# A long convolution with a gate: in the last phase the sums run eight rows ahead of the taps in place of ten

## The chip, the cores and the metric

The kernel runs on one core of one Trainium2 chip. The metric is the device time of one execution in microseconds (us); the time given for a kernel is the median of its timed runs. A profiled execution of its own gives the trace, with times from the start of the span.

## The reference

```
# attention part: u = x*v is convolved along the sequence (12800 long) with a filter from a small MLP
h_filt = (np.maximum(pos_emb @ w1, 0.0) @ w2) * np.exp(-0.01 * pos)[:, None]
y = irfft(rfft(x * v, n=2*S, axis=1) * rfft(h_filt, n=2*S, axis=0), n=2*S, axis=1)[:, :S]
x = x * y                                    # (4, 12800, 128)
# gate part, five taps along the sequence
xp = np.concatenate([np.zeros((B, 4, D)), x], axis=1)
gate_pre = sum(conv_w[k] * xp[:, k:k + S] for k in range(5))
return ((1 / (1 + np.exp(-gate_pre))) * (x @ w_val)) @ w_out
```

## The kernel before

Three phases stand one behind the other. The first transforms the input and the filter, the second multiplies the spectra and goes halfway back, and both leave their results in DRAM. The last phase, from about 684 us to the end, is the one that the change touches: it finishes the inverse transform row by row, multiplies with x, and runs the gate part. The sequence is cut in 2 halves (`j`) of 64 rows; a row is a tile of 128 channels x 400 values (4 batches x 100 positions). Four rows are a group; there are 32 groups (`t` = 0 to 31, `g` = 0 to 15 in each half), so 128 rows.

The order of all instructions on each engine is the order of the program text (`tc.manual_schedule()`): one loop over steps `i`, with `t, r = divmod(i, 4)`, so that a step is "row r of group t" for the taps. One step issues, in this order:

- `y_trans` (TensorE, then ScalarE): four transposes of a summed row into PSUM (`tp`, L684), and two ScalarE copies from it (`dif`, L686 and L687);
- `value` (TensorE, L728) for row r of group t-1, then `finish_last` (ScalarE copy `o_sb`, L746) and `project_last` (TensorE, L738) for the rows ahead of it;
- in even steps `y_sum` for two rows (TensorE, `sd`, L672);
- `tap(t, r + 1)` (VectorE, L716): `gt` = `ext` rows * weight + `gt`, 128x1600, over the four rows that end with row r of group t;
- `gated` (VectorE, `gd`, L733), the value row times the sigmoid;
- `y_join`: VectorE adds `tp` and `dif` to `yr` (L697), and GpSimd multiplies `yr` with x into a row of the buffer `ext` (L699);
- `y_copy` (ScalarE, `sd_sb`, L677);
- at certain r, on ScalarE: `fill_halo` (L655 to L657 or L659), `tap(t + 1, 0)` (L713, 128x1600), and at r = 3 `sigmoid(t)` (`sg`, L721).

`LEAD` sets how many steps the sums stand ahead: row number n (counted in the order in which rows are summed) is summed at step n - LEAD, and transposed and joined two steps later (`LAG`). The rows are summed with the last group of a half first (it goes to the buffer `tail`), so row r of group t is row number 4(t + 1) + r, but for the last group of each half.

`ext` is a buffer of 20 rows, two in turn: 4 rows of halo, then the 16 rows of four groups. Taps 0 to 4 of a group read `ext` rows that start k = 0 to 4 rows below its own; so the first group of a buffer reads the halo rows, which are the last four rows of the buffer before. `fill_halo` copies these on ScalarE (L659, 128x1600) for the second to fourth buffer of a half; for the first of a half it builds them from the tails in three or four smaller copies.

Of the kernel before, what the change touches and what calls it, by code (L numbers as in the profile page):

```python
# [29 lines left out]
R = 4  # L30
# [88 lines left out]
def tile_longconv_gate(  # L119
# [326 lines left out]
    def load_part(s, c, i):  # L446
        j, g = y_order[s]
        if (s, c) not in rows_in:
            rows_in[s, c] = buffer(NP + 1 + s)
        k0, n, step, p0 = PARTS[i]  # L450
        to = rows_in[s, c][p0:p0 + step * (n - 1) + 1:step]
        m, n0 = divmod(g * R, H2)
        if j == 0:
            n0 += m * N2 + c * H2
            nc.sync.dma_start(out=to, in_=c_y[k0:k0 + n, n0:n0 + R].rearrange("k p e -> k (p e)"))
        else:
            if m:
                n0 = H2 - R - n0
            nc.sync.dma_start(
                out=to.rearrange("k (q f) -> k q f", q=2),  # L460
                in_=c_z[k0:k0 + n, m, :, c, n0:n0 + R].rearrange("k q i e -> k q (i e)"))
# [152 lines left out]
    with tc.tile_pool(name="p3", bufs=1, reuse_waits="tile") as p3, \  # L614
# [4 lines left out]
        EG = 4  # L619
        assert HALO == R  # L620
        groups = [(j, g) for j in range(J) for g in range(NG)]
        tails, exts, loads3, sds, tps, gate_sg, gate_gt, outs3 = {}, {}, {}, {}, {}, {}, {}, {}

        def load_x(s):
            j, g = y_order[s]
            xr = p3.tile([D, R * ROW], F32, name="xr", bufs=3)
            nc.sync.dma_start(out=xr, in_=xt[j][:, g * R:(g + 1) * R].rearrange("d n b a -> d (n b a)"))
            loads3[s] = xr

        def load_rows(s, parts):  # L630
            for c in range(2):
                for i in parts:
                    load_part(s, c, i)
            if s not in loads3:
                load_x(s)
# [7 lines left out]
        def new_ext(j, q):  # L643
            e = p3.tile([D, HALO + EG * R, B, N1], F32, name="ext", bufs=2)
            exts[j, q] = e
# [15 lines left out]
        def y_sum(s, r):  # L661
            sd = ps3.tile([128, B * D], F32, name="sd", bufs=2)
            j, g = y_order[s]
            m = g * R // H2
            for c in range(2):
                to, t = sd[c * N2:(c + 1) * N2], rows_in[s, c]
                if j == 0:
                    t = t[:, r * B * D:(r + 1) * B * D]
                else:
                    t = t.rearrange("k (q i e) -> k q i e", q=2, i=R)[:, :, R - 1 - r if m else r]  # L670
                    to = to.rearrange("k (q e) -> k q e", q=2)
                nc.tensor.matmul(out=to, lhsT=inv[:, 2 if j * m * c else c], rhs=t, start=True, stop=True)  # L672
            sds[s, r] = sd
# [6 lines left out]
        def y_trans(s, r):  # L680
            t = sds.pop((s, r))
            tp = ps3.tile([D, B, 128], F32, name="tp3", bufs=2)
            for b in range(B):
                nc.tensor.transpose(out=tp[:, b], in_=t[:, b], identity=ident)  # L684
            dif = p3.tile([D, B, 2, NH], F32, name="dif", bufs=3)
            nc.scalar.copy(out=dif[:, :, 0], in_=tp[:, :, N2:N2 + NH])  # L686
            nc.scalar.activation(dif[:, :, 1], tp[:, :, N2 + 1:N2 + NC1], AF.Copy, scale=-1.0)  # L687
            tps[s, r] = tp, dif
# [11 lines left out]

        def rows(t, k=HALO):
            j, g = groups[t]
            e = exts[j, g // EG].rearrange("d n b a -> d (n b a)")
            r0 = g % EG * R + k
            return e[:, r0 * ROW:(r0 + R) * ROW]

        ALL, TWO = slice(0, R * ROW), (slice(0, 2 * ROW), slice(2 * ROW, R * ROW))
# [1 line left out]
        def tap(t, k, cols=ALL):  # L709
            if k == 0:  # L710
                gt = p3.tile([D, R * ROW], F32, name="gt", bufs=2)
                gate_gt[t] = gt
                nc.scalar.activation(gt, rows(t, 0), AF.Copy, scale=cw[:, 0:1])  # L713
            else:
                gt = gate_gt[t][:, cols]
                nc.vector.scalar_tensor_tensor(gt, rows(t, k)[:, cols], cw[:, k:k + 1], gt, op0=ALU.mult, op1=ALU.add)  # L716
# [6 lines left out]
        def value(t, r):  # L723
            if t == NT - 1 and r >= 2:
                v_ps = ps3.tile([128, B * D], F32, name="sd", bufs=2)[:, 0:ROW]
            else:
                v_ps = ps3.tile([D, ROW], F32, name="v_ps", bufs=2)
            nc.tensor.matmul(out=v_ps, lhsT=wval, rhs=rows(t)[:, r * ROW:(r + 1) * ROW], start=True, stop=True)  # L728
            return v_ps
# [21 lines left out]
                nc.scalar.dma_start(  # L751
                    out=out[j][:, g * R + r0:g * R + r1].rearrange("d n b a -> d (n b a)"), in_=o_sb[:, r0 * ROW:r1 * ROW])

        NT, LEAD, LAG = len(groups), 10, 2
        y_run, gd_last, o_last = [], None, None

        def project_last():
            nonlocal gd_last, o_last
            if gd_last is not None:
                o_last = gd_last[0], gd_last[1], project(gd_last[2])  # L760
                gd_last = None

        def finish_last():
            nonlocal o_last
            if o_last is not None:
                finish(*o_last)
                o_last = None

        with tc.manual_schedule():
            load_x(0)  # L770
            for c, i in ((0, 2), (1, 2)):
                load_part(0, c, i)
            for c, i in ((0, 1), (1, 1), (0, 2), (1, 2)):
                load_part(1, c, i)
            load_x(1)
            for c, i in ((0, 1), (0, 2), (1, 0), (1, 1), (1, 2)):
                load_part(2, c, i)
            load_x(2)

            for i in range(-LEAD, (NT - 1) * R):  # L780
                t, r = divmod(i, R)
                s, q = divmod(i + LEAD, R)
                if q == 0 and s < NT:
                    if 3 <= s + 1 < NT:
                        load_rows(s + 1, (0, 1, 2))
                    j, g = y_order[s]
                    if g == NG - 1:
                        tails[j] = p3.tile([D, R, B, N1], F32, name="tail", bufs=2)
                    elif g % EG == 0:
                        new_ext(j, g // EG)  # L790
                done = y_run.pop(0) if len(y_run) == LAG or s >= NT and y_run else None
                if done:
                    y_trans(*done)
                v_ps = value(t - 1, r) if t >= 1 else None
                finish_last()
                project_last()
                if s < NT and q % 2 == 0:
                    y_sum(s, q)
                    y_sum(s, q + 1)
                if t >= 0:  # L800
                    tap(t, r + 1)
                if v_ps is not None:
                    gd_last = t - 1, r, gated(t - 1, r, v_ps)
                if done:
                    y_join(*done)
                if s < NT:
                    y_copy(s, q)
                    y_run.append((s, q))
                if t + 1 >= 0:
                    j, g = groups[t + 1]  # L810
                    if r == 0 and g == NG - 1:
                        nc.scalar.copy(out=exts[j, g // EG][:, EG * R:], in_=tails[j])
                    if r == 1 and g % EG == 0:
                        fill_halo(j, g // EG)
                    if r == 2:
                        tap(t + 1, 0)
                if t >= 0 and r == R - 1:
                    sigmoid(t)

            t = NT - 1  # L820
            v_last = []
            for i, (h, k) in enumerate((h, k) for h in range(2) for k in range(1, KC)):
                if i < R:
                    v_ps = value(t - 1, i)
                finish_last()
                project_last()
                if i in (R, R + 1):
                    v_last += [value(t, len(v_last)), value(t, len(v_last) + 1)]
                tap(t, k, TWO[h])
                if i < R:  # L830
                    gd_last = t - 1, i, gated(t - 1, i, v_ps)
                elif i in (6, 7):
                    gd_last = t, i - 6, gated(t, i - 6, v_last[i - 6])
                if k == KC - 1:
                    sigmoid(t, TWO[h])
            finish_last()
            project_last()
            for r in (2, 3):
                gd_last = t, r, gated(t, r, v_last[r])
                finish_last()  # L840
                project_last()
            finish_last()
# [41 lines left out]
```

## Time and profile before

| | |
|---|---|
| median of 3 timed runs | 1064.03 us (1063.89 to 1065.49) |
| the profiled execution's own time | 1066.52 us |
| its span in the trace | 1064.7 us |
| mean granted clock of TensorE | 0.976 |
| busy, share of the span: TensorE / VectorE / GpSimd / ScalarE | 92% / 91% / 70% / 61% |
| median to profiled execution | the median is 2.49 us below it |

The busy shares are averages over three phases. What this change is worth is read from the last phase alone. A record's length is not always the distance to the next one on its engine: VectorE and ScalarE start an instruction a little before the record of the one ahead has ended, so steps are measured here from start to start.

### The profile page before, as it was taken

The numbers are of one execution on the slowest core, as the hardware profiler recorded it, in microseconds if no ns is written. First come the engines' busy times: TensorE is split into PE (matmuls) and PEld (weight loads), VectorE is DVE, ScalarE is ACT, GpSimd is POOL, SyncE is SP. The second block draws the span as 40 slices with busy tenths as digits, with TensorE's granted clock in tenths as the row PEclk, the third lists the DMA queues.
The fourth block names the chain that finished last, engine by engine and source line by source line (L and its number), as shares of the span: only waits on it lengthen the run. The fifth ranks groups of instructions, "written<-read, shape, count | busy, mean of one in ns | idle before, by whom it ended". The sixth has DMA issues, their size and how long they took to land.

```text
span 1064.7 us, 21554 instructions
## 1 busy us (share of the span) xinstructions
PE 978.8 (92%) x8100; PEld 515.6 (48%) x8100; DVE 966.9 (91%) x933; ACT 649.2 (61%) x1145; POOL 747.9 (70%) x465
## 2 busy tenths in 40 slices
PE   2778799999988999999999999689999999999996
PEld 0344466566644545555445545334444444444442
DVE  8878999699948999999989999369999999999997
ACT  1445577788852444444444434277887888878784
POOL 2232222222225999999899999679999999999990
PEclk9989899999997999999999999899999999999999
DMA  8999899988989889989999997977888888888813
GB/s 286 383 352 375 330 381 373 397 315 327 393 273 306 318 302 334 341 314 339 333 311 342 345 334 259 333 285 270 312 286 300 284 295 306 282 299 296 299 72 124
DMA packets 97152, 330.16 MB, mean 310 GB/s; under 512 B 12691, under 2 KB 37883, under 8 KB 81051
## 3 DMA queue, kind: packets, MB, share of 16 engines
q1 hardware_dynamic: 41864, 196.96, 54.1%
q10 hardware_dynamic: 49506, 111.30, 27.0%
q0 software_dynamic: 5680, 20.53, 5.1%
q8 instruction: 66, 1.08, 0.4%
q14 instruction: 36, 0.29, 0.1%
HBM read 197.67 MB, written 131.07 MB: 309 GB/s over the span
## 4 chain that ended last, share of the span: by engine, by line
PE 65%; DMA 13%; DVE 7%; POOL 5%; ACT 4%; issue 4%; SPq 1%; ACTq 1%; DVEq 0%; POOLq 0%
PE sd L672 11%; PE o_ps L738 8%; PE v_ps L728 7%; PE c_ps L531 7%; PE fp L392 6%; PE tp L684 6%; PE c_ps L508 6%; PE z_ps L492 5%; DMA xv<-in_xv_dram 4%; DMA ld<-in_xv_dram 3%; PE gp L293 3%; PE ap L267 3%; DMA c_z<-c_both 2%; DVE vb L498 2%; POOL c_both L543 2%
## 5 line engine op out<-in xcount | busy, mean ns | idle before, releaser
L699 POOL TENSOR_TENSOR ext<-yr,xr 128x400 f32<-128x400 f32 x120 | 308.3, 2570 | 23.2 <-DVE yr L697 10.8
L716 DVE SCALAR_TENSOR_TENSOR gt<-ext,cw,gt 128x1600 f32<-128x1600 f32 (+1 forms) x132 | 242.3, 1835 | 0.1
L401 POOL DMA_DIRECT2D a_u<-st x62 | 33.3, 537 | 222.9 <-ACT st L393 219.1
L393 ACT COPY st<-fp 128x1024 f32<-128x1024 f32 x124 | 125.7, 1029 | 81.6 <-PE fp L392 41.4
L672 PE MATMUL sd<-ld,inv 128*64 128x512 f32 x512 | 128.0, 619 | 7.2 <-DMA ld<-c_y 6.7
L543 POOL TENSOR_TENSOR c_both<-c_raw 128x512 f32<-128x512 f32 x100 | 126.6, 1295 | 9.9 <-DMA c_z<-c_both 6.4
L536 ACT COPY c_raw<-c_ps 128x1024 f32<-128x1024 f32 x50 | 50.8, 1015 | 135.3 <-PE c_ps L531 117.9
L498 DVE TENSOR_TENSOR va<-z_ps,h_sb 128x2048 f32<-128x2048 f32 x50 | 114.1, 2282 | 19.7 <-PE z_ps L492 19.6
L579 POOL TENSOR_TENSOR va<-va,vb 128x1024 f32<-128x1024 f32 x49 | 117.0, 2387 | 20.4 <-DVE vb L498 20.4
L498 DVE TENSOR_TENSOR vb<-z_ps,h_sb 128x2048 f32<-128x2048 f32 x50 | 114.2, 2284 | 12.8 <-POOL va L582 12.8
L492 PE MATMUL z_ps<-ld,ld 64*64 64x512 f32 x800 | 111.6, 614 | 10.2 <-DVE vb L498 6.1
L392 PE MATMUL fp<-ld,fsd 64*128 64x512 f32 x320 | 89.4, 663 | 27.3 <-DVE ld L343 14.5
L738 PE MATMUL o_ps<-gd,wout 128*128 128x400 f32 x256 | 107.8, 503 | 6.1 <-DVE gd L733 4.6
L677 ACT COPY sd_sb<-sd 128x512 f32<-128x512 f32 x128 | 76.9, 601 | 49.4 <-PE sd L672 37.8
L728 PE MATMUL v_ps<-ext,wval 128*128 128x400 f32 x252 | 105.4, 501 | 0.0
L508 PE MATMUL c_ps<-va,ld 64*64 64x512 f32 x800 | 98.1, 604 | 4.0 <-POOL va L579 2.5
L582 POOL TENSOR_TENSOR va<-va,vb 128x1024 f32<-128x1024 f32 x42 | 101.0, 2406 | 0.0
L684 PEld LDWEIGHTS tp<-ident,sd_sb 128*128 128x128 f32 x512 | 58.3, 140 | 77.8 <-PE sd L672 45.4
L697 DVE TENSOR_TENSOR yr<-tp,dif 128x400 f32<-128x400 f32 x128 | 72.5, 566 | 25.8 <-ACT dif L687 21.6
L514 ACT COPY c_sb<-c_ps 128x1024 f32<-128x1024 f32 x49 | 49.7, 1014 | 59.5 <-PE c_ps L508 59.5
L684 PE MATMUL tp<-ident,sd_sb 128*128 128x128 f32 x512 | 80.0, 280 | 4.0 <-DVE yr L697 4.0
L733 DVE TENSOR_TENSOR gd<-v_ps,sg 128x400 f32<-128x400 f32 x126 | 71.4, 567 | 0.2 <-ACT sg L721 0.2
(116 smaller groups left out, 1817.7 us busy)
## 6 DMA issues: line engine op xcount, KB each, us to landing
ld<-a_u SPq DMA_DIRECT2D x48, 1024.0 KB
a_u<-st ACTq DMA_DIRECT2D x61, 512.0 KB
xr<-in_xt_dram SPq DMA_DIRECT2D x32, 800.0 KB
c_y<-c_sb ACTq DMA_DIRECT2D x49, 512.0 KB
out_dram<-o_sb ACTq DMA_DIRECT2D x31, 800.0 KB
c_z<-c_both ACTq DMA_DIRECT2D x48, 512.0 KB
ld<-in_xv_dram SPq DMA_DIRECT2D x40, 512.0 KB
ld<-c_y SPq DMA_DIRECT2D x32, 512.0 KB
```

What stands on the lines that cost most here:

```text
L392: nc.tensor.matmul(out=fp[:, j], lhsT=fsd[h, c], rhs=both[c][h], start=True, stop=True)
L393: nc.scalar.copy(out=st[:, c], in_=fp.rearrange("k j e -> k (j e)"))
L492: nc.tensor.matmul(out=z[half[h], c], lhsT=wk[half[c], 0, half[h]], rhs=a2[half[c], h, j], start=True, stop=True)
L498: nc.vector.tensor_tensor(out, z.rearrange("p (b d) -> p b d", d=D).unsqueeze(1).to_broadcast([128, n, B, D]), h_sb.unsqueeze(2).to_broadc ...
L508: nc.tensor.matmul(out=c_ps[half[m], h], lhsT=wk[half[h], 1 + c, half[m]], rhs=vt[half[h], c].rearrange("p b d -> p (b d)"), start=(c == 0 ...
L543: nc.gpsimd.tensor_tensor(both[:, :, m], raw[:, :, 1], raw[:, :, 0], op=op)
L672: nc.tensor.matmul(out=to, lhsT=inv[:, 2 if j * m * c else c], rhs=t, start=True, stop=True)
L684: nc.tensor.transpose(out=tp[:, b], in_=t[:, b], identity=ident)
L699: nc.gpsimd.tensor_tensor(e[:, r0 + r], yr, xr, op=ALU.mult)
L716: nc.vector.scalar_tensor_tensor(gt, rows(t, k)[:, cols], cw[:, k:k + 1], gt, op0=ALU.mult, op1=ALU.add)
L728: nc.tensor.matmul(out=v_ps, lhsT=wval, rhs=rows(t)[:, r * ROW:(r + 1) * ROW], start=True, stop=True)
L738: nc.tensor.matmul(out=o_ps, lhsT=wout, rhs=gd, start=True, stop=True)
```

## The change

The sums stand 8 steps ahead of the taps. Tap 0 of the first group of a second to fourth buffer reads its four rows from the end of the old buffer, where they were written, and no longer from the copied halo. The halo copy stands at r = 3 (at r = 2 for the first buffer of the second half, at r = 1 at the very start) in place of r = 1.

```diff
         def rows(t, k=HALO):
             j, g = groups[t]
-            e = exts[j, g // EG].rearrange("d n b a -> d (n b a)")
-            r0 = g % EG * R + k
+            q, r0 = g // EG, g % EG * R + k
+            if r0 == 0 and q > 0:
+                q, r0 = q - 1, EG * R
+            e = exts[j, q].rearrange("d n b a -> d (n b a)")
             return e[:, r0 * ROW:(r0 + R) * ROW]
...
-        NT, LEAD, LAG = len(groups), 10, 2
+        NT, LEAD, LAG = len(groups), 8, 2
...
-                    if r == 1 and g % EG == 0:
+                    if g % EG == 0 and r == (1 if t < 0 else 2 if g == 0 else 3):
                         fill_halo(j, g // EG)
```

What it moves is seen on three places; in brackets stand the engines that an instruction waits for (the numbers at the end of a name in brackets are those of semaphores). L716, L721, L733, L746 and L713 of before are L718, L723, L735, L748 and L715 of the change. First VectorE in the middle of the phase, the steps r = 3 to r = 2 around the start of a group, before:

```order
L716 SCALAR_TENSOR_TENSOR gt<-ext,cw,gt 128x1600 [waits DVE_49]
L733 TENSOR_TENSOR gd<-v_ps,sg 128x400 [waits PE_49]
L697 TENSOR_TENSOR yr<-tp_6733,dif 128x400 [waits Activation_49,Pool_49]
L716 SCALAR_TENSOR_TENSOR gt<-ext,cw,gt 128x1600
L733 TENSOR_TENSOR gd<-v_ps,sg 128x400 [waits PE_49,Activation_49]
L697 TENSOR_TENSOR yr<-tp_6756,dif 128x400 [waits Activation_49,Pool_49]
```

and now, the last tap here being the first one behind a halo copy:

```order
L718 SCALAR_TENSOR_TENSOR gt<-ext,cw,gt 128x1600 [waits DVE_49,Pool_49]
L735 TENSOR_TENSOR gd<-v_ps,sg 128x400 [waits PE_49]
L697 TENSOR_TENSOR yr<-tp_6773,dif 128x400 [waits Activation_49]
L718 SCALAR_TENSOR_TENSOR gt<-ext,cw,gt 128x1600 [waits DVE_49,Pool_49]
L735 TENSOR_TENSOR gd<-v_ps,sg 128x400 [waits PE_49]
L697 TENSOR_TENSOR yr<-tp_6803,dif 128x400 [waits Activation_49]
L718 SCALAR_TENSOR_TENSOR gt<-ext,cw,gt 128x1600 [waits Activation_49,Pool_49]
```

The order of tap, gated row and join is the same; the wait for GpSimd has gone from `yr`, which stood last in a step, to the tap, which stands first in it, and the tap behind a halo copy waits for ScalarE too. Second, ScalarE where the first such halo copy stands, steps r = 1 to r = 3, before:

```order
L677 COPY sd_sb<-sd 128x512
L659 COPY ext<-ext 128x1600 [waits DMASW2_49,Pool_49]
L686 COPY dif<-tp_6814 128x4x50 [waits DVE_49,PE_49]
L687 ACTIVATE dif<-tp_6814 128x4x50
L746 COPY o_sb<-o_ps 128x400
L677 COPY sd_sb<-sd 128x512 [waits PE_49]
L713 ACTIVATE gt<-ext,cw 128x1600 [waits Activation_49]
L686 COPY dif<-tp_6844 128x4x50 [waits DVE_49,PE_49]
L687 ACTIVATE dif<-tp_6844 128x4x50
L746 COPY o_sb<-o_ps 128x400
L677 COPY sd_sb<-sd 128x512
L721 ACTIVATE sg<-gt 128x1600 [waits DVE_49]
```

and now, steps r = 2 and r = 3 of the same group:

```order
L677 COPY sd_sb<-sd 128x512 [waits PE_49]
L715 ACTIVATE gt<-ext,cw 128x1600 [waits Pool_49]
L686 COPY dif<-tp_6803 128x4x50 [waits DVE_49,PE_49]
L687 ACTIVATE dif<-tp_6803 128x4x50
L748 COPY o_sb<-o_ps 128x400
L677 COPY sd_sb<-sd 128x512
L659 COPY ext<-ext 128x1600 [waits DMASW2_49]
L723 ACTIVATE sg<-gt 128x1600 [waits DVE_49]
```

The halo copy L659 now stands behind tap 0 and the whole ScalarE work of step r = 3, ahead of the sigmoid, and tap 0 waits for GpSimd. Third, VectorE where the taps begin, before (the memset is part of the first halo):

```order
L697 TENSOR_TENSOR yr<-tp_6401,dif 128x400 [waits PE_49,Activation_49,Pool_49]
L652 MEMSET ext 128x16
L697 TENSOR_TENSOR yr<-tp_6426,dif 128x400 [waits PE_49,Activation_49,Pool_49]
L697 TENSOR_TENSOR yr<-tp_6447,dif 128x400 [waits PE_49,Activation_49,Pool_49]
L716 SCALAR_TENSOR_TENSOR gt<-ext,cw,gt 128x1600 [waits DVE_49]
```

and now:

```order
L697 TENSOR_TENSOR yr<-tp_6369,dif 128x400 [waits PE_49,Activation_49,Pool_49]
L652 MEMSET ext 128x16
L697 TENSOR_TENSOR yr<-tp_6386,dif 128x400 [waits PE_49,Activation_49,Pool_49]
L697 TENSOR_TENSOR yr<-tp_6407,dif 128x400 [waits PE_49,Activation_49,Pool_49]
L718 SCALAR_TENSOR_TENSOR gt<-ext,cw,gt 128x1600 [waits Pool_49]
```

Six joined rows stand ahead of the first tap in place of eight. The number of instructions of each kind is the same.

## Rows read from the trace of the kernel before

**Rows 1.** Middle of the last phase: engines' busy time, TensorE's granted clock, DMA share.

```profile
core 0: us, PE busy (x) PEld busy (x) DVE busy (x) ACT busy (x) POOL busy (x), PEclk, DMA share, GB/s
717.20:1037.20 320.00, 318.82 (x1367) 154.51 (x1366) 319.36 (x346) 256.66 (x526) 300.09 (x115) 1.00 0.79 275
```

**Rows 2.** Chain that ended last, from 690 us on: start us, us, what.

```profile
720.51 1.87 PE sd L672 x8
...
971.71 1.87 PE sd L672 x8
```

**Rows 3.** Groups of VectorE instructions, 717.2 to 1037.2 us: count, busy, mean ns, idle before.

```profile
L716 DVE SCALAR_TENSOR_TENSOR gt<-ext,cw,gt 128x1600 f32<-128x1600 f32 x115 | 215.6, 1874 | 0.0
L697 DVE TENSOR_TENSOR yr<-tp,dif 128x400 f32<-128x400 f32 x116 | 65.6, 566 | 0.6 <-ACT dif L687 0.3 <-ACT o_sb L746 0.2
```

**Rows 4.** Timeline of VectorE over one step: start us, us, instruction.

```profile
755.78 1.87 DVE L716 SCALAR_TENSOR_TENSOR gt<-ext,cw,gt 128x1600 f32<-128x1600 f32 x1
757.57 0.56 DVE L733 TENSOR_TENSOR gd<-v_ps,sg 128x400 f32<-128x400 f32 x1
758.06 0.56 DVE L697 TENSOR_TENSOR yr<-tp,dif 128x400 f32<-128x400 f32 x1
758.54 1.87 DVE L716 SCALAR_TENSOR_TENSOR gt<-ext,cw,gt 128x1600 f32<-128x1600 f32 x1
```

**Rows 5.** Timeline of GpSimd and VectorE, a step in the middle of the phase.

```profile
717.16 1.87 DVE L716 SCALAR_TENSOR_TENSOR gt<-ext,cw,gt 128x1600 f32<-128x1600 f32 x1
717.32 2.61 POOL L699 TENSOR_TENSOR ext<-yr,xr 128x400 f32<-128x400 f32 x1 [0.15 <-DVE yr L697]
719.92 1.87 DVE L716 SCALAR_TENSOR_TENSOR gt<-ext,cw,gt 128x1600 f32<-128x1600 f32 x1
```

**Rows 6.** Timeline of the second phase: a VectorE instruction that waited for GpSimd.

```profile
623.07 2.41 POOL L582 TENSOR_TENSOR va<-va,vb 128x1024 f32<-128x1024 f32 x1
625.51 2.29 DVE L498 TENSOR_TENSOR vb<-z_ps,h_sb 128x2048 f32<-128x2048 f32 x1 [1.18 <-POOL va L582]
```

**Rows 7.** Timeline of ScalarE, steps r = 2 and r = 3 of the group of rows 4.

```profile
755.57 1.63 ACT L713 ACTIVATE gt<-ext,cw 128x1600 f32<-128x1600 f32 x1
757.90 0.62 ACT L677 COPY sd_sb<-sd 128x512 f32<-128x512 f32 x1
758.38 1.58 ACT L721 ACTIVATE sg<-gt 128x1600 f32<-128x1600 f32 x1
```

**Rows 8.** Timeline of ScalarE: the first halo copy L659, at r = 1.

```profile
741.66 1.53 ACT L659 COPY ext<-ext 128x1600 f32<-128x1600 f32 x1
```

**Rows 9.** Timeline where the second half begins: halo copies on ScalarE, and VectorE.

```profile
875.62 0.22 ACT L654 COPY ext<-tail 128x16 f32<-128x16 f32 x1
877.37 0.32 ACT L686 COPY dif<-tp 128x200 f32<-128x200 f32 x1
878.03 0.57 DVE L697 TENSOR_TENSOR yr<-tp,dif 128x400 f32<-128x400 f32 x1 [0.26 <-ACT dif L687]
```

**Rows 10.** Timeline where the taps begin: GpSimd, ScalarE, VectorE.

```profile
696.34 1.04 POOL L699 TENSOR_TENSOR tail<-yr,xr 128x400 f32<-128x400 f32 x1 [0.90 <-DMA ld<-c_y]
698.84 0.88 ACT L655 COPY ext<-tail 128x784 f32<-128x784 f32 x1
704.10 1.87 DVE L716 SCALAR_TENSOR_TENSOR gt<-ext,cw,gt 128x1600 f32<-128x1600 f32 x1
714.10 2.17 DVE L716 SCALAR_TENSOR_TENSOR gt<-ext,cw,gt 128x1600 f32<-128x1600 f32 x1
```

**Rows 11.** Timeline of VectorE and GpSimd where the joins end.

```profile
1037.23 1.88 DVE L716 SCALAR_TENSOR_TENSOR gt<-ext,cw,gt 128x1600 f32<-128x1600 f32 x1
1037.39 2.61 POOL L699 TENSOR_TENSOR ext<-yr,xr 128x400 f32<-128x400 f32 x1 [0.15 <-DVE yr L697]
1039.51 2.17 DVE L716 SCALAR_TENSOR_TENSOR gt<-ext,cw,gt 128x1600 f32<-128x1600 f32 x1
1042.09 1.87 DVE L716 SCALAR_TENSOR_TENSOR gt<-ext,cw,gt 128x1600 f32<-128x1600 f32 x1
```

## The prediction, made before the change was run

> **What bounds the kernel now.** The view by stages comes first: from 717 to 1037 us TensorE and VectorE are both busy all the time, GpSimd for 300 of 320 us, ScalarE for 257, and TensorE's granted clock is 1.00, its level of 2.4 GHz [rows 1]. Three engines this close together leave little room for a wait. The chain that ended last tells which one leads: the sums `sd` return in it at even distances, from 720.51 to 971.71 us in 45 equal pieces, 5.582 us for two rows, so TensorE needs 2.791 us a row [rows 2]. The groups of VectorE have 0.6 us of idle time in the same 320 us [rows 3], so VectorE is nearly as tight: its own step, tap to tap, takes 758.54 - 755.78 = 2.76 us [rows 4]. Counted over the stage, the taps from 717.16 [rows 5] to 1037.23 us [rows 11] are 115 steps in 320.07 us, 2.783 each. What lies behind 1037 us is VectorE alone, taps and gated rows with no join between. So the end is set by VectorE: by when the taps begin, by the steps with a join, by the steps without one. Whatever holds a tap, and is not won back by a faster VectorE step, is paid at the end.
>
> **What the change does to the waits.** A tap of step i reads a row whose join was issued in step i - 4 before, and is issued in step i - 2 now (row number i + 4 is joined at step n - LEAD + 2). Between that `yr` and the tap stands one whole step of VectorE. GpSimd's part of the join is not fast: it starts 0.16 us after a tap has started and lasts 2.61 us, that is to 2.77 us after the tap's start; the next tap starts at 2.76 us [rows 5]. Alone, the same product takes 1.04 us [rows 10]; it gets on while VectorE is not in a tap. So the join of step i - 2 ends just when tap i would start. Before, nobody wanted it then: `yr` wanted its buffer back two thirds of a step later.
>
> **A. Every tap waits for GpSimd.** The hand-over from GpSimd to VectorE is seen where a VectorE instruction of the second phase truly waited: the product's record ends at 623.07 + 2.41 = 625.48 us, the waiting one starts at 625.51, 0.03 us later [rows 6]. Tap to tap becomes 2.77 + 0.03 = 2.80 us. That is a little above TensorE's 2.791, so TensorE stops leading, and the waits for it, which make 2.783 out of 2.76 now, are no longer paid on top. Two more steps have a join (120 rows are left to join behind the first tap now, 122 then): 117 x 2.80 = 327.6 us in place of 320.07, **+7.5 us**. Bounds: no price at all, 117 x 2.76 = 322.9 us, +2.9; and if each step costs 0.05 us more, half of the lead of 0.11 us that the tap still has over the next join, +13.4.
>
> The end at 2.77 us is the term to doubt. A join that got nothing done until the record of the tap has ended would take its 1.04 us [rows 10] from 1.87 us on and end at 2.91; a step would be 2.94 and part A 117 x 2.94 - 320.07 = +23.9 us. The row ends it at 2.77 [rows 5], and the sum keeps the row. The Trainium skill, "SBUF — State Buffer", section "SBUF: two separate sides", says that VectorE and GpSimd share a port pair under an exclusive lock: an instruction with two SBUF inputs that starts first holds it to its end. By that, part A would be +23.9; the trace agrees that a join hardly moves beside a tap, but not with so late an end.
>
> **B. The halo copy is late, six times.** The second to fourth buffer of each half have a halo copy L659. It stands at r = 3 now, and the first tap behind it is the first thing that VectorE does in the next step. Ahead of it on ScalarE stands tap 0, which reads the last row of its group; that row's join is issued at r = 1 now and ends, by the sum above, as VectorE reaches step r = 3. So tap 0 starts with the tap of r = 3 (before, 755.57 against 755.78: 0.21 us ahead [rows 4, 7]). From tap 0 to where the sigmoid stands behind `dif`, `o_sb` and `sd_sb`, ScalarE takes 758.38 - 755.57 = 2.81 us [rows 7]; there the halo copy begins now, and lasts 1.53 us [rows 8]. With 0.03 us for the hand-over the tap starts 2.81 + 1.53 + 0.03 = 4.37 us after the tap ahead of it, in place of 2.80: 1.57 us late. The step behind is free of its wait for GpSimd (the join had the pause to finish in) and gives 0.04 back: 1.53 us. Six times: **+9.2 us**. None of it is hidden: VectorE has no idle time to put it in, and its step is not shorter than TensorE's afterwards, so nothing catches up. Before, at r = 1, the same copy had two steps more, and VectorE, idle for 0.6 us in all, shows no such gap [rows 3]. Behind it on ScalarE is queued the sigmoid, for the gated rows of the next step: it ends 1.58 us after the halo copy, and the gated row stands 1.79 us behind the late tap [rows 4, 7], so it is not late again. In the other groups the sigmoid ends 2.81 + 1.58 = 4.39 us behind tap 0's start, the gated row stands at 2.80 + 1.79 = 4.59, so that tap 0's new wait costs nothing there.
>
> **C. The second half's first buffer.** Its four copies take 877.37 - 875.62 = 1.75 us of ScalarE [rows 9], now ahead of tap 0 in r = 2. Then the `dif` copies of step r = 3 come late for its `yr`: the copies begin 0.2 us ahead of the tap of r = 3, where tap 0 stands now, or up to 0.8 ahead should TensorE's sum come earlier (my estimate); 1.75 us for them and about 2.1 for tap 0 and two `dif` copies (most of the 2.33 to `sd_sb` [rows 7]) leave `yr` at 3.1 to 3.7 us in place of 758.06 - 755.78 = 2.28 [rows 4], 0.8 to 1.4 late. Before, it was 0.26 late [rows 9], inside the 320.07. **+1.1 us**.
>
> **D. The start.** The first halo's copies wait for the fourth joined row, done at 696.34 + 1.04 = 697.38 us; before they stood at 698.84 behind two more rows [rows 10]. The same work follows up to the first tap, so it starts 1.4 us earlier than 704.10. But the first four taps have no gated rows; 10.00 us for four of them [rows 10] become 4 x 2.80 = 11.2, since each waits for a join. Of 1.4 us there is left **-0.3 us** (bounds -1.4 and +0.3).
>
> **E. The tail.** Two steps with tap and gated row alone are gone; one takes 1039.51 - 1037.23 = 2.28 us [rows 11]: **-4.6 us**.
>
> Sum: 7.5 + 9.2 + 1.1 - 0.3 - 4.6 = +12.9 us. The profiled execution, 1066.52 us for a span of 1064.7, lies 2.49 us above the median; the difference is carried to the median: 1064.03 + 12.9 = 1077 us, a profiled span near 1077.6.
>
> **Rivals.** (1) The wait for GpSimd is free and VectorE wins back on TensorE: steps of 2.76 us, +2.9, with smaller halo stalls (tap 0 at its old place, 1.36 us each, 8.2 in all), +0.8 in C, -1.4 at the start: +5.9 us, 1070. For it: VectorE's floor is below TensorE's pace. Against: the join ends 0.01 us behind the tap that will wait for it [rows 5].
> (2) The wait changes who gets in first. Where a tap starts while a join is still running it takes 2.17 us in place of 1.87 [rows 11]. If the joins come to start ahead of the taps, every step is 0.3 us longer than 2.76: 117 x 0.26 over part A, +30 us more, 1107. Half of the steps so would give 1092. Against: the join still starts 0.11 us behind the tap (0.16 less the 0.05 that the tap slips).
> (3) Faster: the halo stall is not there. The place is L659 on ScalarE at r = 3; it decides whether tap 0 can start 1.57 us ahead of the tap of r = 3. Then only A, D and E count: at today's 2.783 a step, 5.5 - 1.4 - 4.6 = -0.5 us, no change; at 2.76, 2.9 - 1.4 - 4.6 = -3.1 us, 1061. Against: tap 0 now waits for a join that ends only there.
> (4) The join ends 2.91 us behind the tap's start, as worked out in A: 23.9 in place of 7.5, 1093. Against: the row. It is the lock of the skill's page taken to the letter.
> (5) Halo stalls as in B, but TensorE and VectorE alternate in leading and a step is 2.783: +10.9, 1075, which is inside the forecast.
>
> **Chances.** The forecast with (5), 1072 to 1082 us: 0.66. Rival (1): 0.14. Rivals (2), 0.08, and (4), 0.03. Rival (3): 0.05 faster, 0.04 within 0.2% (2.1 us, about what a measurement of this kernel can tell). Slower: 0.91. A range of 1069 to 1083 takes in the forecast, rival (1) and the lower bounds of A and B, and leaves out some 0.18.
>
> **What would show it.** Right: VectorE's taps wait for GpSimd in the list of waits, in nearly every step with a few hundredths of a microsecond; distance tap to tap 2.80; six gaps of about 1.5 us in front of a tap, released by ScalarE's `ext` L659; one gap before `yr` near the second half's start; TensorE idle 0.5 to 1 us behind each; first tap near 702.7 us. Wrong: no gap at the six places (B), taps of 2.17 us in the middle of the phase (A too low), a tap distance of 2.76 (A too high), or a tail no shorter than 27 us (E).

## The result

The changed kernel takes 1080.04 us (median of 3 runs, 1075.90 to 1080.38) against 1064.03 us: 1.0133 times the time before, with an interval of 1.0104 to 1.0162. It is slower by 16.0 us; the interval, taken of 1064.03 us, runs from 11.1 to 17.2 us. The forecast was 12.9 us and 1077, with a range of 1069 to 1083.

Its profiled execution took 1075.90 us, with a span of 1074.1. Single executions of one kernel lie several microseconds apart (in the later comparisons the kernel before had runs from 1058.84 to 1070.40 us), and most of that comes from the first two phases, which no kernel here changes: in the eleven traces the first sum of the last phase starts anywhere from 677.35 to 688.10 us. So traces are compared from the first sum of the last phase to the end of the span. The first sum of the kernel before, in its timeline of TensorE:

```profile
684.87 4.19 PE L672 MATMUL sd<-ld,inv 128*64 128x512 f32 x8 [6.68 <-DMA ld<-c_y]
```

and that of the changed one:

```profile
677.35 4.06 PE L672 MATMUL sd<-ld,inv 128*64 128x512 f32 x8 [6.76 <-DMA ld<-c_y]
```

From there to the end it is 1064.7 - 684.87 = 379.8 us before and 1074.1 - 677.35 = 396.75 us after, 16.9 us more. Such a stretch is good to about 1 us: from the first sum to the first tap, kernels that are the same up to there take 17.39 to 18.62 us with a lead of eight (the change, e2, e3, e9, e11) and 18.64 to 19.23 with a lead of ten (before, e1, e6). By the terms of the prediction (steps are distances from tap to tap in the timeline of VectorE; `after` has 117 of them between the sixth tap and the end of the joins, six behind a halo copy, one at the second half's start, 110 others with a mean of 2.811 us):

| term | forecast | measured | from |
|---|---|---|---|
| A, every step longer | +7.5 | +8.8 | 117 x 2.811 - 320.07 |
| B, six late halo copies | +9.2 | +10.0 | six steps, 26.85 us in all, less 6 x 2.811 |
| C, start of the second half | +1.1 | +1.7 | one step of 4.50, less 2.811 |
| D, start of the taps | -0.3 | +0.7 | first sum to sixth tap, 33.00 for 32.29 |
| E, tail | -4.6 | -4.3 | last tap with a join to the end, 23.16 for 27.47 |
| sum | +12.9 | +16.9 | |

No term made up for another: each came out dearer than forecast, by 0.3 to 1.3 us.

The stage between those taps answers to [rows 1]. TensorE was busy for 318.82 of 320 us before; now it stands still for 12 us of 344:

```profile
707.00:1050.90 343.90, 331.75 (x1399) 153.10 (x1396) 331.99 (x355) 267.91 (x541) 304.00 (x118) 1.00 0.70 261
```

One halo copy in the timeline of the changed kernel, from the step ahead of r = 3 on; it answers to [rows 4, 5, 7, 8]:

```profile
735.69 1.89 DVE L718 SCALAR_TENSOR_TENSOR gt<-ext,cw,gt 128x1600 f32<-128x1600 f32 x1
735.80 2.67 POOL L699 TENSOR_TENSOR ext<-yr,xr 128x400 f32<-128x400 f32 x1
...
737.97 0.57 DVE L697 TENSOR_TENSOR yr<-tp,dif 128x400 f32<-128x400 f32 x1
...
738.50 1.63 ACT L715 ACTIVATE gt<-ext,cw 128x1600 f32<-128x1600 f32 x1 [0.57 <-POOL ext L699]
738.50 1.89 DVE L718 SCALAR_TENSOR_TENSOR gt<-ext,cw,gt 128x1600 f32<-128x1600 f32 x1
...
741.32 1.55 ACT L659 COPY ext<-ext 128x1600 f32<-128x1600 f32 x1
742.75 1.57 ACT L723 ACTIVATE sg<-gt 128x1600 f32<-128x1600 f32 x1
742.98 1.89 DVE L718 SCALAR_TENSOR_TENSOR gt<-ext,cw,gt 128x1600 f32<-128x1600 f32 x1 [1.62 <-ACT ext L659]
...
745.49 0.91 PE L740 MATMUL o_ps<-gd,wout 128*128 128x400 f32 x2 [0.41 <-DVE gd L735]
...
745.75 1.88 DVE L718 SCALAR_TENSOR_TENSOR gt<-ext,cw,gt 128x1600 f32<-128x1600 f32 x1
```

GpSimd's product ends at 735.80 + 2.67 = 738.47; 0.03 us later both the tap of VectorE and tap 0 of ScalarE start. That is the ordinary step: 738.50 - 735.69 = 2.81 us. Then the halo copy starts 2.82 us behind tap 0, lasts 1.55, and the next tap begins 4.48 us after the one ahead, in place of 2.81. TensorE waits for the gated row behind it.

The list of VectorE's waits, 700 to 1060 us (in all, times, longest):

```profile
DVE gt L718 <- ACT ext L659: 9.7, 6, 1.6
DVE yr L697 <- ACT dif L687: 1.7, 1, 1.7
DVE gt L718 <- POOL ext L699: 1.3, 3, 0.4
DVE gd L735 <- ACT sg L723: 0.7, 2, 0.5
```

B and C stand there as forecast. A does not: only three waits for GpSimd are listed, all at the two ends of the phase. VectorE starts a tap before the record of the `yr` ahead of it has ended (738.50 against 737.97 + 0.57 = 738.54); in an ordinary step now it starts 0.05 us later than it could, still inside that record, so there is no idle time to list. The wait shows in the distance of the taps, and in where they start: of the 112 taps from the seventh to the 118th, 95 start 0.03 to 0.04 us behind the end of a product. In the kernel before none does, and the median is 0.01 us ahead of it. The kernel holds its own comparison. Shortly before the second half, the joined rows are those of a tail, which no tap needs soon:

```profile
867.24 1.88 DVE L718 SCALAR_TENSOR_TENSOR gt<-ext,cw,gt 128x1600 f32<-128x1600 f32 x1
867.36 10.96 POOL L699 TENSOR_TENSOR tail<-yr,xr 128x400 f32<-128x400 f32 x4
870.01 1.88 DVE L718 SCALAR_TENSOR_TENSOR gt<-ext,cw,gt 128x1600 f32<-128x1600 f32 x1
872.77 1.88 DVE L718 SCALAR_TENSOR_TENSOR gt<-ext,cw,gt 128x1600 f32<-128x1600 f32 x1
```

These steps take 2.77 and 2.76 us with the same work on both engines: 0.05 us a step is the price of the wait.

Where the second half begins (C), the copy L655 of the tail waits for the last join of that tail and starts 0.06 us behind the tap of 878.29; tap 0 and the `dif` copies stand behind the copies, and `yr` waits for them:

```profile
878.35 0.86 ACT L655 COPY ext<-tail 128x784 f32<-128x784 f32 x1 [0.31 <-POOL tail L699]
...
882.30 0.58 DVE L697 TENSOR_TENSOR yr<-tp,dif 128x400 f32<-128x400 f32 x1 [1.66 <-ACT dif L687]
```

Where the taps begin, which answers to [rows 10], the first tap comes 695.30 - 677.35 = 17.95 us behind the first sum, 1.3 less than before, as forecast. But the next five steps take 15.05 us for 13.06:

```profile
695.30 1.88 DVE L718 SCALAR_TENSOR_TENSOR gt<-ext,cw,gt 128x1600 f32<-128x1600 f32 x1
695.46 3.60 POOL L699 TENSOR_TENSOR ext<-yr,xr 128x400 f32<-128x400 f32 x2 [1.42 <-DVE yr L697]
698.11 2.64 DVE L718 SCALAR_TENSOR_TENSOR gt<-ext,cw,gt 128x1600 f32<-128x1600 f32 x1 [0.44 <-POOL ext L699]
701.15 1.87 DVE L718 SCALAR_TENSOR_TENSOR gt<-ext,cw,gt 128x1600 f32<-128x1600 f32 x1
...
703.95 1.63 ACT L715 ACTIVATE gt<-ext,cw 128x1600 f32<-128x1600 f32 x1 [3.54 <-POOL ext L699]
...
709.38 0.57 DVE L735 TENSOR_TENSOR gd<-v_ps,sg 128x400 f32<-128x400 f32 x1 [0.51 <-ACT sg L723]
```

Two products stand back to back here: the second was waiting when the first ended, started a little ahead of the tap, and the tap took 2.64 us in place of 1.88. The same stands at 703.95. That is the mechanism of rival (2), at two steps of the whole kernel. The last of the five steps takes 3.35 us for 3.06 before: tap 0 now waits 3.54 us for its join, the sigmoid stands behind it on ScalarE, and the first gated row waits 0.51 us for the sigmoid.

At the end, which answers to [rows 11], one tap without a join still has to wait for the last join, and has no `yr` to hide it: its step takes 1053.75 - 1050.94 = 2.81 us where the prediction kept 2.58:

```profile
1050.94 1.89 DVE L718 SCALAR_TENSOR_TENSOR gt<-ext,cw,gt 128x1600 f32<-128x1600 f32 x1
...
1053.75 1.89 DVE L718 SCALAR_TENSOR_TENSOR gt<-ext,cw,gt 128x1600 f32<-128x1600 f32 x1 [0.43 <-POOL ext L699]
```

### The profile page after: what moved, and what is told of

The parts are those of the page before. It is cut to its first block, busy times and chain, and to the rows that moved or that the text cites. A ratio compares the mean times of both kernels' runs of the same rounds, so it can differ in the third digit from the quotient of the medians.

```text
span 1074.1 us, 21566 instructions
## 1 busy us (share of the span) xinstructions
PE 981.6 (91%) x8100; PEld 510.7 (48%) x8100; DVE 971.0 (90%) x933; ACT 651.7 (61%) x1145; POOL 743.8 (69%) x465
## 4 chain that ended last, share of the span: by engine, by line
PE 57%; DMA 12%; DVE 10%; POOL 6%; issue 6%; ACT 6%; SPq 1%; ACTq 0%; POOLq 0%; DVEq 0%
PE sd L672 9%; PE c_ps L531 8%; PE o_ps L740 6%; PE c_ps L508 6%; PE z_ps L492 6%; PE v_ps L730 5%; PE fp L392 5%; DMA ld<-in_xv_dram 5%; PE tp L684 4%; PE gp L293 2%; DMA xv<-in_xv_dram 2%; DVE vb L498 2%; DVE gt L718 2%; PE ap L267 2%; POOL va L582 2%
## 5 line engine op out<-in xcount | busy, mean ns | idle before, releaser
L699 POOL TENSOR_TENSOR ext<-yr,xr 128x400 f32<-128x400 f32 x120 | 304.4, 2537 | 48.2 <-DVE yr L697 36.1
L718 DVE SCALAR_TENSOR_TENSOR gt<-ext,cw,gt 128x1600 f32<-128x1600 f32 (+1 forms) x132 | 243.4, 1844 | 11.1 <-ACT ext L659 9.7
L740 PE MATMUL o_ps<-gd,wout 128*128 128x400 f32 x256 | 111.3, 517 | 15.9 <-DVE gd L735 13.4
L740 PEld LDWEIGHTS o_ps<-gd,wout 128*128 128x128 f32 x256 | 42.6, 189 | 67.8 <-ACT o_sb L748 27.9
```

The source lines that it names most:

```text
L699: nc.gpsimd.tensor_tensor(e[:, r0 + r], yr, xr, op=ALU.mult)
L740: nc.tensor.matmul(out=o_ps, lhsT=wout, rhs=gd, start=True, stop=True)
```

## The experiments

The theory: two things cost time, the distance from a join to the tap that reads its row (A), and the place of the halo copy in ScalarE's order (B, C). Rivals: the smaller lead of the sums costs by itself; the gaps come from tap 0's wait or from the port that GpSimd and VectorE share; the longer step is no wait. "Ratio" is the ratio to runs of the kernel before on the same chip, "phase" is from the first sum to the end in the trace, "step" the mean distance of taps outside the seven long steps, which are those at the six halo copies and the one at the start of the second half (a range where single steps differ; for the kernel before and e8 the mean of all steps), "gap" the distance of the taps at the six halo copies.

| kernel | lead | ratio (interval) | phase, us | step, us | gap, us |
|---|---|---|---|---|---|
| before | 10 | | 379.8 | 2.783 | none |
| the change | 8 | 1.0133 (1.0104 to 1.0162) | 396.75 | 2.811 | 4.47 to 4.48 |
| e1, late halo alone | 10 | 1.0073 (1.0045 to 1.0100) | 387.4 | 2.759 | 4.07 to 4.40 |
| e2, lead alone | 8 | 1.0209 (1.0173 to 1.0246) | 403.0 | 2.81 to 2.82 | 5.32 to 5.33 |
| e3, split halo | 8 | 1.0103 (1.0064 to 1.0141) | 393.4 | 2.81 to 2.82 | 3.47, then 3.06 |
| e7, split halo | 9 | 1.0030 (1.0001 to 1.0059) | 382.7 | 2.76 | 3.04 to 3.36, then 3.15 to 3.48 |
| e8, early rows | 9 | 0.9985 (0.9965 to 1.0006) | 379.3 | 2.783 | none |
| e9, early rows | 8 | 1.0058 (1.0031 to 1.0085) | 388.1 | 2.81 to 2.82 | 2.82, then 3.00 |
| e10 | 7 | one run, 1221.23 us | 532.8 | 4.00 | 4.47 to 4.82 |
| e6, join first | 10 | 1.0547 (1.0510 to 1.0584) | 437.4 | 3.28 | none |
| e11, early rows, join first | 8 | 1.0565 (1.0535 to 1.0595) | 441.5 | 3.28 | none |

**e1: the other two edits with the old lead.** The change with

```diff
-        NT, LEAD, LAG = len(groups), 8, 2
+        NT, LEAD, LAG = len(groups), 10, 2
```

> The sums stay ten rows ahead, the other two edits are kept. Theory (the joins are too close to the taps, and the halo copy at r = 3 stands behind a step's work of ScalarE): no tap waits for GpSimd, tap to tap is back at 2.78 us on average; the six taps behind a halo copy are still late, by 1.4 to 1.8 us each, since 2.81 + 1.53 us of ScalarE lie between tap 0 and them; 7 to 10 us over the kernel before, about 1072 us. Rival (the late taps come from the smaller lead of the sums, through tap 0's wait for the join): no gaps at the halo copies, within 0.2% of the kernel before.

It differs from the change by this number alone. The gaps stay (first the list of waits below, 710 to 1060 us, then one place in the timeline), and so does the wait of `yr` where the second half begins, so the copies are late by their own place, with tap 0 free to start 0.34 us ahead of the tap of r = 3:

```profile
DVE gt L718 <- ACT ext L659: 8.6, 6, 1.6
DVE yr L697 <- ACT dif L687: 1.6, 1, 1.6
```

```profile
747.24 1.63 ACT L715 ACTIVATE gt<-ext,cw 128x1600 f32<-128x1600 f32 x1
...
747.58 1.86 DVE L718 SCALAR_TENSOR_TENSOR gt<-ext,cw,gt 128x1600 f32<-128x1600 f32 x1
...
750.05 1.56 ACT L659 COPY ext<-ext 128x1600 f32<-128x1600 f32 x1
...
751.65 1.89 DVE L718 SCALAR_TENSOR_TENSOR gt<-ext,cw,gt 128x1600 f32<-128x1600 f32 x1 [1.24 <-ACT ext L659]
```

And the ordinary step is 2.759 us, shorter than the 2.783 of the kernel before: its steps of 2.85 to 2.89 us, one in four over long stretches, are gone here, as they would be if TensorE gets ahead while VectorE stands at a halo copy. Without a wait for GpSimd, part of each gap is won back; in the change, with 2.811, nothing but 0.04 us in the step behind is. The rival falls. The hand-over is shorter here: the tap starts 0.04 us behind the end of the halo copy (0.03 at the other five places) where it took 0.10 to 0.11 in the change.

**e2: the lead alone.** The kernel before with `LEAD` 8 for 10.

> Only the lead is changed, 8 for 10; tap 0 reads the copied halo, the copy stands at r = 1. Theory: ScalarE's copy at r = 1 waits for a join issued in the same step, which ends a step and a half later, and the dif copies of r = 2 stand behind it; so yr of r = 2 is 2 to 3 us late at six places, and every tap waits for GpSimd as in the change: 18 to 22 us over the kernel before, 1082 to 1086 us, slower than the change. Rival (the two edits on the halo are what costs): at most 9 us over the kernel before, faster than the change.

The phase is 23.2 us longer than before, a little over the range expected and 6.3 us over the change. At r = 1 the halo copy waits for a join issued in its own step, and the `dif` copies of the next step are queued behind it:

```profile
741.97 1.52 ACT L659 COPY ext<-ext 128x1600 f32<-128x1600 f32 x1 [3.29 <-POOL ext L699]
...
743.99 0.57 DVE L697 TENSOR_TENSOR yr<-tp,dif 128x400 f32<-128x400 f32 x1 [2.46 <-ACT dif L687]
```

So with a lead of 8 the two halo edits are a gain, of 1.0 us or so at each place; they only do not repay what the lead costs.

**e3: the halo copied row by row.** In the change:

```diff
-                    if g % EG == 0 and r == (1 if t < 0 else 2 if g == 0 else 3):
-                        fill_halo(j, g // EG)
+                    if g == 0 and r == (1 if t < 0 else 2):
+                        fill_halo(j, 0)
+                    if g % EG == 0 and g > 0 and r > 0:
+                        nc.scalar.copy(out=exts[j, g // EG][:, r:r + 1], in_=exts[j, g // EG - 1][:, EG * R + r:EG * R + r + 1])
```

> The change, but the halo copy is cut in rows: row r of the halo is copied at step r (1, 2, 3), 128x400 each; halo row 0, which no tap reads any more, is not copied. Theory: behind tap 0 there is a copy of 0.5 us in place of 1.55, so each of the six taps is 0.5 to 0.6 us late in place of 1.66; the wait of every tap for GpSimd stays at 2.81 us a step; 6 to 7 us under the change, 9 to 10 over the kernel before, 1073 to 1074 us. Rival (the gaps come from the port that GpSimd and VectorE share, or from tap 0's wait): gaps stay near 1.6 us.

The gap shrinks nearly as expected, to 3.47 - 2.81 = 0.66 us, which is 6.0 us at six places, but the phase shrinks only by 3.3 us in place of 6 to 7. Of the rest, 1.7 us are given back in the step behind, which takes 3.06 us for 2.77 in the change:

```profile
745.57 3.79 POOL L699 TENSOR_TENSOR ext<-yr,xr 128x400 f32<-128x400 f32 x2 [0.20 <-DVE yr L697]
...
748.22 0.56 ACT L818 COPY ext<-ext 128x400 f32<-128x400 f32 x1
...
748.87 2.17 DVE L718 SCALAR_TENSOR_TENSOR gt<-ext,cw,gt 128x1600 f32<-128x1600 f32 x1 [0.62 <-ACT ext L818]
...
751.93 1.87 DVE L718 SCALAR_TENSOR_TENSOR gt<-ext,cw,gt 128x1600 f32<-128x1600 f32 x1
```

The two products end at 749.36; the tap starts at 748.87, in the middle of the second, and takes 2.17 us in place of 1.88. The pause of the change, 1.6 us, was long enough for that product to finish first; a pause of 0.6 us is not. The last 0.9 us lie ahead of the sixth tap (0.7) and behind the last join (0.2), where the two kernels are the same.

**e7: the same with a lead of nine.** e3 with `LEAD` 9.

> The split halo copy, and the sums nine rows ahead: three steps lie between a join and the tap that reads it, in place of two. Theory: the taps' wait for GpSimd is gone, tap to tap 2.78 to 2.79 us (TensorE's pace); the six taps are at most 0.5 us late; 0 to 3 us over the kernel before, 1064 to 1067 us. Rival (the slower step is not the wait for the join): tap to tap stays at 2.81 us, 5 us over the kernel before or more.

With three steps between a join and its tap the ordinary step is 2.76 us, so the wait A is gone; the phase is 2.9 us over the kernel before, as expected. But the six places are 1.0 us late each, over two steps, and not 0.5 at most: as in e3, a tap waits for the row of r = 3, starts in the middle of a product, and takes 2.26 to 2.59 us.

```profile
742.48 6.50 POOL L699 TENSOR_TENSOR ext<-yr,xr 128x400 f32<-128x400 f32 x3 [0.19 <-DVE yr L697]
...
748.08 2.58 DVE L718 SCALAR_TENSOR_TENSOR gt<-ext,cw,gt 128x1600 f32<-128x1600 f32 x1 [0.21 <-ACT ext L818]
```

With the start of the second half that is 7.1 us; the ordinary step, 2.758 us for 2.783, gives part of it back.

**e8: nine ahead, the halo rows in ScalarE's idle time.** In the change, with `halo_rows(at, a, b)` copying rows a to b - 1 of a halo at step r = at:

```diff
-        NT, LEAD, LAG = len(groups), 8, 2
+        NT, LEAD, LAG = len(groups), 9, 2
...
+                halo_rows(1, 1, 3)
                 if s < NT:
                     y_copy(s, q)
                     y_run.append((s, q))
+                halo_rows(1, 3, 4)
...
-                    if g % EG == 0 and r == (1 if t < 0 else 2 if g == 0 else 3):
-                        fill_halo(j, g // EG)
+                    if g == 0 and r == 1:
+                        fill_halo(j, 0)
```

> Nine rows ahead; the halo of a second to fourth buffer is copied at r = 1, rows 1 and 2 ahead of the sd_sb copy and row 3 behind it, in time that ScalarE spends waiting for TensorE; the first buffer's halo of the second half stands at r = 1 again. Theory: no tap waits for a halo copy, none for GpSimd, tap to tap is TensorE's 2.78 us; from the first sum to the end 377 to 380 us (379.8 in the kernel before), so 0 to 3 us under the kernel before, 1061 to 1064 us on its scale. Rival (a smaller lead costs by itself, whatever becomes of the halo): 2 us over the kernel before or more.

None of the six places has a longer step than its neighbours (at the start of the second half one step takes 3.06 us, 3.11 in the kernel before), no tap waits for GpSimd, and the mean step is 2.783 us, as in the kernel before. The phase is 0.5 us shorter, which is less than traces differ by; the ratio's interval holds 1. So a lead of nine costs nothing by itself, and it gains nothing that can be measured.

**e9: eight ahead, early rows.** The change with halo rows 1 and 2 at r = 2 ahead of `y_copy`, and row 3 at r = 3 right behind `y_trans`:

```diff
                 if done:
                     y_trans(*done)
+                halo_rows(3, 3, 4)
...
+                halo_rows(2, 1, 3)
                 if s < NT:
                     y_copy(s, q)
...
-                    if g % EG == 0 and r == (1 if t < 0 else 2 if g == 0 else 3):
-                        fill_halo(j, g // EG)
+                    if g == 0 and r == (1 if t < 0 else 2):
+                        fill_halo(j, 0)
```

> The change with its lead of eight, but halo rows 1 and 2 copied at r = 2 ahead of the sd_sb copy, and row 3 at r = 3 right behind the dif copies, so that it is done before the step ends. Theory: the gaps behind the halo copies are gone or under 0.3 us, the wait of each tap for GpSimd stays, 2.81 us a step; from the first sum to the end 386 to 389 us, 6 to 9 us over the kernel before. Rival (the halo copy only takes the blame for a wait that tap 0 causes): gaps of 0.6 us or more stay.

The six gaps are gone but for 0.2 us in the step behind, the phase is 8.6 us under the change, and the step keeps its 2.81 us. What is left over the kernel before, 8.3 us, is A, C and D less E, with the 0.2 us at six steps. A and B are thus two separate costs.

**e10: seven ahead.** The change with `LEAD` 7 and the first halo of each half at r = 2. A tap then waits for the join issued in the step just ahead of it.

> The change with the sums seven rows ahead: the join that a tap waits for is the one issued in the step just ahead of it (the first halo of all stands one step later). Theory (a tap waits for the end of its join): a step is VectorE's 2.28 us to yr, 0.56 of yr, 0.08 to GpSimd, 1.03 for the product alone and 0.03 back, 3.98 us; 140 to 150 us over the kernel before, about 1210 us; the gaps at the halo copies shrink to some 0.4 us. Rival (the steps of 2.81 us come from GpSimd and VectorE using SBUF together, not from the wait): a step stays under 3.1 us.

The step is 4.00 us; the sum of the parts was 3.98. In the timeline a step is `yr`, the product alone, and 0.04 us later the tap (the first three lines). The phase is 153 us longer than before, over the 140 to 150 expected, for at the start of the second half one step takes 8.54 us, with `yr` waiting for `dif` (the last line):

```profile
802.91 0.56 DVE L697 TENSOR_TENSOR yr<-tp,dif 128x400 f32<-128x400 f32 x1
...
803.55 1.03 POOL L699 TENSOR_TENSOR ext<-yr,xr 128x400 f32<-128x400 f32 x1 [2.96 <-DVE yr L697]
804.62 1.88 DVE L718 SCALAR_TENSOR_TENSOR gt<-ext,cw,gt 128x1600 f32<-128x1600 f32 x1 [1.14 <-POOL ext L699]
...
959.27 0.57 DVE L697 TENSOR_TENSOR yr<-tp,dif 128x400 f32<-128x400 f32 x1 [4.40 <-ACT dif L687]
```

By the steps that lie between a join and its tap, a step costs 2.76 us (three, e7), 2.81 (two), 4.00 (one). Four of its steps, where the joins go to the tail of the second half, take 2.76 us each here too.

**e11 and e6: the join ahead of the gated row.** e9, and the kernel before as a control, with

```diff
+                if done:
+                    y_join(*done)
                 if v_ps is not None:
                     gd_last = t - 1, r, gated(t - 1, r, v_ps)
-                if done:
-                    y_join(*done)
```

> As the kernel with early halo rows and a lead of eight, and in every step the join stands ahead of the gated row on VectorE. Theory: GpSimd's product gets on during the gated row that follows yr, so it ends about 0.3 us before the tap that wants it; no tap waits for GpSimd any more, and a step is TensorE's 2.79 us, from the first sum to the end about 385 us, 2 to 3 us less than with the gated row first. Rival (yr, now 0.48 us earlier in the step, waits for ScalarE's dif copies): yr waits in most steps, a step is 2.85 us or more, 392 us or more. Second rival (the 2.81 us are not the wait): a step stays at 2.81 us.

> The kernel before with the join ahead of the gated row on VectorE, as a control. Theory: no tap waited for GpSimd in the kernel before, so there is nothing to gain; within 2 us of the kernel before, or slower if yr comes to wait for the dif copies. Rival (the order of join and gated row matters by itself): 3 us or more under the kernel before.

Neither the theory nor the rivals of these two runs had this: both phases are 57 to 62 us longer than the one before, with a step of 3.28 us. That is over the 2.85 us of e11's first rival, but not for its reason: `yr` waits four times, 4.1 us in all. What happens stands in the timeline of e11:

```profile
800.30 0.56 DVE L697 TENSOR_TENSOR yr<-tp,dif 128x400 f32<-128x400 f32 x1
800.78 0.56 DVE L735 TENSOR_TENSOR gd<-v_ps,sg 128x400 f32<-128x400 f32 x1
800.94 1.05 POOL L699 TENSOR_TENSOR ext<-yr,xr 128x400 f32<-128x400 f32 x1 [2.24 <-DVE yr L697]
801.26 2.40 DVE L718 SCALAR_TENSOR_TENSOR gt<-ext,cw,gt 128x1600 f32<-128x1600 f32 x1
...
804.56 2.39 DVE L718 SCALAR_TENSOR_TENSOR gt<-ext,cw,gt 128x1600 f32<-128x1600 f32 x1
```

With the gated row behind `yr`, the product starts 0.32 us ahead of the tap. It then takes 1.05 us, as if alone, and the tap 2.40. In the old order the tap is first by 0.16 us, takes its 1.87, and the product 2.61. Who starts first decides who waits, and here it must be the tap.

## Why the prediction was right, and where it was off

**A** held: the join two steps ahead ends when the tap wants to start, and the tap follows 0.03 us behind it. The size was a little low, 2.811 for 2.80 us: the product starts 0.11 us behind the tap in place of 0.16, and yet ends 738.47 - 735.69 = 2.78 us behind the tap's start, no earlier than the 2.77 before. Over 117 steps that is the 1.3 us by which A was short. What was wrong is how it would show: not as waits in the list, but as a longer distance from tap to tap with no idle time beside it. That it is the wait follows from e1, which differs by the lead alone, from the steps that join into the tail, and from e10. (One reading beside the sum is off: the old wait of `yr` for its buffer stood 2.27 us behind the product's end by [rows 4, 5], four fifths of a step and not two thirds.)

**The rule weighed in A.** The prediction found that its trace agreed with the blocking but not with so late an end. The runs let that be read more closely: a product that starts behind a tap ends 2.77 us after the tap's start, which is 1.03 us, its time alone, behind a point 1.74 us after the tap's start, 0.13 us before the tap's record ends; and a product that starts first takes its 1.05 us while the tap grows by 0.52 (e11). The Trainium skill's rule in "SBUF — State Buffer", "SBUF: two separate sides", that the first of the two holds the port pair for its whole instruction, agrees with both cases. What was off was taking the end of a tap's record for the end of its hold. The tap in e11 is blocked for less than the record of the product says, too: 0.73 us of it are left at the tap's start, and the tap grows by 0.53. Why the holds end 0.13 and 0.2 us ahead of the records is not shown.

**B** held in place, number and mechanism; 1.66 us each for 1.57, mostly since the hand-over from ScalarE to VectorE takes 0.11 us (742.98 less 742.87) where the one from GpSimd, 0.03, had been put in. It is not a price of ScalarE as such: in e1, where this tap waits for ScalarE alone and not for GpSimd too, it took 0.03 to 0.04. That no more than the 0.04 us of the step behind is won back held in the change; e1 shows that it is won back in part where A is absent.

**C** was low, 1.7 for 1.1 us. ScalarE took longer from the start of the copies to `yr`, 4.07 us (884.20 to 888.27 in e1) for the 1.75 and 2.1 of the sum, and the copies stand later than the 0.2 to 0.8 us ahead of the tap that had been put in: in the change L655 waits 0.31 us for the last join of the tail. That wait is not all of it. In e1 the joins are done in time, the copies start only 0.14 us ahead of the tap, since ScalarE was waiting for a sum of TensorE, and the step is 1.66 us longer than the others; in e7 they start 0.68 us ahead, and it is 1.15.

**D** had the wrong sign, +0.7 for -0.3. The first tap came 1.3 us earlier, near the 1.4 worked out. The first four steps behind it took 11.7 us for 11.2, because products stand back to back there and get in ahead of two taps, and the fifth, which the term left as it was, 0.3 us more, for the sigmoid. The term had priced the wait, but neither the port nor what tap 0's wait does to the first gated row. The size is no better than the 1 us of such a stretch; the sign is the same in all traces, 31.71 to 32.29 us from the first sum to the sixth tap with a lead of ten, 32.45 to 33.67 with eight.

**E** was right but for 0.2 us, the last join's wait.

**Rivals.** (2) is a true mechanism, and a dear one: 0.5 us a step in e6 and e11. It did not come about in the middle of the change, since the product still starts behind the tap there. (1), (3) and (5) fell with the step and the gaps; (4) with the step.

## What to carry to other kernels

A buffer of steps between a producer and its reader can be smaller than it looks where the producer is itself held up: before cutting it, compare the producer's end with the start of the reader that will now need it, not with the one that needs it today. A step that is some hundredths of a microsecond longer with no idle time listed is still a wait; look at start-to-start distances, and for a stretch of the same work that does not depend on the producer. And when a copy is moved later to let its input be ready, count everything that stands ahead of it on its own engine against the time until its first reader: copies fitted into that engine's idle time took the gaps away without a change in what is computed.

## What was not expected of the hardware

Two instructions that both took their own time in one order cost 0.5 us a step in the other: exchanging a 0.56 us gated row and a 0.56 us `yr` on VectorE made a phase of 380 us 57 us longer (e6), because GpSimd's product then starts 0.3 us ahead of VectorE's tap. The tap's length tells how much of a product was left when it started: 1.87 us with none, 2.17 with 0.49 left (e3), 2.40 with 0.73 left (e11), 2.58 with 0.90 left (e7), each 0.2 us less than 1.87 and the rest of the product. And a tap that waited for ScalarE alone started 0.03 us behind the copy (e1, e7), one that waited for ScalarE and GpSimd 0.10 (the change, e3, e10), though the product that it reads had ended 0.4 us before or earlier.
